# Placing other work in the gaps of each attention step by a table, and normalising the first batch on ScalarE

## The chip, the core and the metric

The kernel runs on one core of a Trainium2 chip. The core has five engines with a queue of their own each: TensorE (PE) for matmuls, with its weight loads (PEld) beside them, VectorE (DVE), ScalarE (ACT), GpSimd (POOL) and SyncE (SP), which here only issues DMAs. Each works off its instructions in the order in which the program holds them, and waits on semaphores for what others produce. The metric is the device time of the kernel in microseconds, as the median of several runs.

## What is computed

A linear attention with decay, whose output is laid out as 4 batches of 768 rows by 512 columns, goes through a Fourier mix, a normalisation and two dense layers. Cut to what matters:

```python
# q, k, v: (4, 8, 768, 64); blocks of 64 rows; lam: one decay per head
for b in range(nb):
    intra = einsum(qb, kb) * Dmask            # within a block
    intra = einsum(intra, vb)
    inter = einsum(qb * lam_pow, kv_state)    # from the state
    out[block] = intra + inter
    kv_state = lam_block * kv_state + einsum(kb * rev_pow, vb)
x = out.transpose(0, 2, 1, 3).reshape(4, 768, 512)

mixed = real(fft(fft(x, axis=1), axis=2))
u = x + mixed
un = (u - mean(u)) / sqrt(var(u) + 1e-6)      # over the 512 columns
out = u + maximum(un @ w_ch1, 0) @ w_ch2      # w_ch1: 512 x 2048, w_ch2: 2048 x 512
```

All is in 32 bit floats, but the two weight matrices arrive as 64 bit floats.

## The kernel before

**Attention** runs in 12 steps of 256 rows, three to a batch. A step first makes the scores of its rows (`scores`, L429 on TensorE; VectorE multiplies them by the decay, L435) and the part that comes from the state (`from_state`, L444). Then it transposes keys and queries of the next step (`turn_k` L394, `turn_q` L400, copied out of PSUM by ScalarE at L395 and L401, and scaled by VectorE at L403), turns the output of the step before back into rows (`back`, transposes at L470), updates the state (`to_state`, L409 and, on VectorE, L419) and makes the part within the blocks (`within`, L450, copied out by ScalarE at L456). `attention` is a Python generator: it yields three times in a step, so that other work can be written into the program at these places: behind the scores and ahead of the next transposes, behind these and ahead of `back`, and behind `within` and ahead of the next scores. Below they are the first, second and third gap.

**The mix** of a batch (`fft_ln`) has folds of mirrored rows and columns on VectorE (L598 to L692), matmuls along the sequence (L725, five products of eight TensorE records), and for each of three groups of two row tiles a product along the width (`wide`, L737 to L742), sums of it into the rows (`summed`, L818 to L825), means and variances (`stats`, L756 and L757 on VectorE, L760 and L761 on GpSimd), the normalising (`norm`, L777 on VectorE) and transposes of the normalised rows for the dense layers (L784, copied out at L788). One group ends with one more product for a single row (`width(HC, ...)`). The first batch (`LEADS`) is folded from tiles that attention leaves in SBUF; the others are read back through DRAM, with mirrored rows by gathers (L612, L619).

**The weights** come in 32 chunks of 512 KB. A chunk is converted from 64 to 32 bits by five VectorE instructions (L264, L266, L269, L272, L273) with one of ScalarE among them (L265), in three parts with a yield behind each. Chunks 0 to 7 are the first half of the columns of `w_ch1`, chunks 8 to 15 the half of `w_ch2` that goes with it; then follows the second half.

**The dense layers** of a group and a half of the hidden units (`mlp`) are eight units of four matmuls each for the first layer (L882; the Relu on ScalarE at L890, in the second half every other one on VectorE at L888), and then the second layer (L896), added into the rows at L926 and L927 for the first half and L930 and L931 for the second.

**The order.** Up to `strict[0] = False` instructions marked by `P` or `keep` stay on their engine in the order in which the Python code writes them. It writes attention, the first batch's mix and the weights' conversion as a mixture by weights (`mixed`): each generator has a length in made-up units, and the one that is furthest behind its share goes next. Behind attention come eight first-layer units of group 1 and then eight of group 2, with the rest of the first half of the weights between them. From `strict[0] = False` on a scheduler in the build orders the instructions by its own estimates, within the dependences. The last part (`late`, behind the release of the pools) works on the remaining eight groups and isn't touched.

## Time and profile before

| | |
|---|---|
| median of 3 runs | 786.39 us (785.94 to 786.59) |
| profiled execution | 785.49 us, span 783.6 us |
| granted TensorE clock, mean | 0.993 |
| ScalarE, GpSimd busy | 200.9 us, 189.3 us |
| DMA | 123.49 MB, mean 158 GB/s |

In the rows below a line of a timeline has start, length, engine, source line, operation, output and inputs with their shapes, the number of instructions merged into it, and in brackets the idle time ahead of it with what ended it. A line of a table by stretches has the stretch and its length, then for PE, PEld, DVE, ACT and POOL the busy time with the number of instructions, then the clock that TensorE was granted (1 is full speed), the busy share of the DMA and its GB/s. A line of groups has the busy time and the mean in ns of one instruction, and behind the second bar the idle time ahead of them.

### The profile page before, as it was taken

How to read it: one execution, taken by the hardware profiler on the slowest of the kernel's cores; microseconds unless marked ns; L12 is line 12 of the kernel's file. 1: busy time of each engine (PE TensorE's matmuls, PEld its weight loads, DVE VectorE, ACT ScalarE, POOL GpSimd, SP SyncE). 2: the span in 40 equal slices, each digit the busy share in tenths (PEclk: the TensorE clock that was granted, in tenths of full speed). 3: DMA queues.
4: the chain of work that ended last, by engine and by line, in shares of the span. 5: the costliest groups of instructions: out<-in, count | busy, mean ns of one | idle time of the engine just before them, and what ended most of it. 6: DMA issues, size and time to landing. Idle time of an engine off the chain costs nothing.

```text
span 783.6 us, 17057 instructions
## 1 busy us (share of the span) xinstructions
PE 742.9 (95%) x6872; PEld 645.0 (82%) x6872; DVE 612.8 (78%) x1183; ACT 200.9 (26%) x468; POOL 189.3 (24%) x215
## 2 busy tenths in 40 slices
PE   6899987699999999999899999999999999999997
PEld 5788876587576758659746889999999999999997
DVE  5689866687998858556884999889986699758983
ACT  2454443343132111002101221024311442024310
POOL 3343442310002114210102970360014100230013
PEclk9999999899999999999999999999999999999999
DMA  9879885174352536530350464876545455465442
GB/s 213 249 199 240 228 240 145 47 278 135 86 194 78 96 119 196 121 121 27 68 147 28 148 223 142 264 248 212 173 138 157 151 178 175 129 182 176 138 144 68
DMA packets 132739, 123.49 MB, mean 158 GB/s; under 512 B 67006, under 2 KB 93246, under 8 KB 132662
## 3 DMA queue, kind: packets, MB, share of 16 engines
q1 hardware_dynamic: 126326, 101.56, 45.9%
q0 software_dynamic: 4032, 12.99, 4.7%
q10 hardware_dynamic: 2304, 7.87, 3.1%
q8 instruction: 54, 0.88, 0.5%
q14 instruction: 23, 0.19, 0.1%
HBM read 90.66 MB, written 31.73 MB: 156 GB/s over the span
## 4 chain that ended last, share of the span: by engine, by line
PE 68%; DVE 17%; issue 7%; DMA 4%; POOL 3%; ACT 1%; SPq 0%; DVEq 0%; POOLq 0%; ACTq 0%
PE p L1331 21%; PE p L1257 17%; PE pm L896 7%; PE pm L882 7%; PE p L1164 5%; PE pa L882 2%; PE pa L725 2%; DVE w L273 1%; DVE e L272 1%; DVE w L269 1%; DVE stt L756 1%; PE pa L450 1%; PE pa L429 1%; DMA w<-in_v_dram 1%; PE pm L725 1%
## 5 line engine op out<-in xcount | busy, mean ns | idle before, releaser
L896 PE MATMUL pm<-w,hr 128*128 128x512 f32 x240 | 104.6, 592 | 0.0
L882 PE MATMUL pm<-ut,w 128*128 128x256 f32 x432 | 97.7, 380 | 3.2 <-DVE hr L888 1.5
L882 PEld LDWEIGHTS pm<-ut,w 128*128 128x128 f32 x432 | 81.2, 190 | 18.1 <-issue 3.3
L896 PEld LDWEIGHTS pm<-w,hr 128*128 128x128 f32 x240 | 45.4, 190 | 53.4 <-issue 52.1
L1352 POOL TENSOR_TENSOR y<-y,u 128x512 f32<-128x512 f32 x12 | 19.9, 1661 | 186.8 <-DVE y L1361 155.5
L1331 PE MATMUL p<-tx,sx 128*128 128x128 f32 x400 | 52.7, 275 | 0.0
L1331 PEld LDWEIGHTS p<-tx,sx 128*128 128x128 f32 x400 | 48.6, 192 | 0.0
L1266 DVE TENSOR_TENSOR ha<-p,ha 128x512 f32<-128x512 f32 x60 | 40.1, 685 | 8.3 <-PE p L1257 8.1
L1337 ACT COPY y<-p 128x128 f32<-128x128 f32 x48 | 12.8, 266 | 103.6 <-PE p L1331 103.1
L1339 DVE TENSOR_TENSOR y<-p,y 128x128 f32<-128x128 f32 x92 | 25.6, 285 | 16.1 <-PE p L1331 9.4
L1331 PE MATMUL p<-w,ha 128*128 128x128 f32 x288 | 37.4, 275 | 0.0
L265 ACT ACTIVATE e<-e,cvt 128x512 uint16<-128x512 uint16 x32 | 22.9, 721 | 53.8 <-DVE e L264 53.7
L1266 DVE TENSOR_TENSOR hs<-p,hs 128x512 f32<-128x512 f32 x39 | 26.2, 685 | 12.0 <-PE p L1257 12.0
L1331 PEld LDWEIGHTS p<-w,ha 128*128 128x128 f32 x288 | 34.9, 192 | 0.1
L890 ACT ACTIVATE hr<-pm 128x256 f32<-128x256 f32 x34 | 13.0, 381 | 84.3 <-PE pm L882 83.4
L1257 PE MATMUL p<-sx,tx 128*128 128x128 f32 x264 | 33.9, 275 | 0.0
L871 POOL DMA_INDIRECT out_dram<-y,ix x12 | 13.6, 1130 | 76.0 <-DVE y L931 64.3
L1257 PEld LDWEIGHTS p<-sx,tx 128*128 128x128 f32 x264 | 31.6, 192 | 0.0
L429 PE MATMUL pa<-w 64*64 64x128 f32 x768 | 27.4, 277 | 3.9 <-issue 2.0
L429 PEld LDWEIGHTS pa<-w 64*64 64x64 f32 x768 | 23.5, 136 | 6.3 <-issue 3.2
L1257 PE MATMUL p<-ur,w 128*128 128x128 f32 x216 | 28.0, 275 | 0.0
L612 POOL DMA_INDIRECT fo<-xa,ix x6 | 7.1, 1182 | 86.3 <-PE pa L725 74.0
(334 smaller groups left out, 1923.1 us busy)
## 6 DMA issues: line engine op xcount, KB each, us to landing
tx<-td SPq DMA_DIRECT2D x84, 256.0 KB, 2.9
tx<-sd SPq DMA_DIRECT2D x63, 256.0 KB, 3.0
words<-in_moe_w_ch_dram SPq DMA_DIRECT2D x19, 512.0 KB, 4.2
raw<-in_moe_w_ch_dram ACTq DMA_DIRECT2D x13, 512.0 KB, 7.3
w<-in_v_dram SPq DMA_DIRECT2D x12, 512.0 KB, 4.4
words<-in_k_dram SPq DMA_DIRECT2D x11, 512.0 KB, 6.2
td<-tx SPq DMA_DIRECT2D x21, 256.0 KB, 2.0
ud<-x SPq DMA_DIRECT2D x16, 256.0 KB, 2.2
```

The costliest lines, as they stand in the source:

```text
L265: P(nc.scalar.activation(pw, pw, AF.Relu, bias=cvt[:, 0:1], scale=8.0))
L429: lead(P(mm(pss[r][hi][HD[ch], hp, :], lhsT=kT[HD[hi], r, hp, D * ch:D * ch + D], rhs=qT[HD[hi], hp, C * ch:C * ch + C], start=True, stop= ...
L725: mm = P(nc.tensor.matmul(ps[:, n, :], lhsT=piece(a, i, n), rhs=cs[0:rows, a, i in (2, 3), n, :], start=(a == 0), stop=(a == 1)))
L871: P(nc.gpsimd.indirect_dma_start(out=out_high, out_offset=row_of(2 + HC * (b + 1) + T - HC), in_=y[:, :], in_offset=None))
L882: P(nc.tensor.matmul(ps, lhsT=w1[:, c, 128 * fc:128 * fc + 128], rhs=ut[:, c, :], start=(c == 0), stop=(c == KO - 1)))
L896: return P(nc.tensor.matmul(ps, lhsT=hr[(fc - f0) // 4][:, fc % 4, 128 * i:128 * i + 128], rhs=w2[:, fc, :], start=(fc == f0), stop=(fc == ...
L1164: nc.tensor.matmul(ps, lhsT=s2.A[a][:, kt, 128 * i:128 * i + 128], rhs=U[b][:, kt, :], start=(first and kt == 0), stop=(kt == 1), skip_gro ...
L1257: nc.tensor.matmul(ps[:, 128 * i:128 * i + 128], lhsT=ab[m][0][:, 128 * i:128 * i + 128], rhs=ab[m][1], start=(start and i == 0), stop=Tru ...
L1266: V.tensor_tensor(o, p, o, op=ADD)
L1331: nc.tensor.matmul(ps[:, 0:HM // 2], lhsT=ab[m][0][i], rhs=ab[m][1][:, i, :], start=(start and i == 0), stop=(i == HF // 2 - 1), skip_grou ...
L1339: V.tensor_tensor(o, ps[:, 0:HM // 2], o, op=ADD)
L1352: nc.gpsimd.tensor_tensor(o, y, u, op=ADD)
```

## The change

Five things are changed.

- A table `PLAN` gives for each of the 12 steps three strings, one for each gap. Each letter writes one unit into the gap: `w` the next third of a weight chunk, `m` the next unit of the first batch's mix.
- A string `REST` does the same for the time behind attention; there `l` is a first-layer unit of group 1 and `k` one of group 2. Four `l`, four `k`, four `l` and four `k` stand in it, with the last units of the mix and 22 thirds of chunks between them; seven thirds follow.
- The first batch's mix yields in smaller units in an order of its own: the width product of a group ahead of the norm of the one before, and the norm of a tile and its transposes in two units.
- The first batch's rows are normalised by ScalarE (`activation` with Identity, a scale and a bias for each row) instead of VectorE. GpSimd makes the bias from mean and scale by two more instructions for each group.
- The copies of the first batch's rows out of PSUM in `back` go from VectorE to ScalarE, but for one tile.

```diff
@@ -490,8 +490,11 @@
                 if not last:
                     x = xn_[b, c] = new(xp, [C, DM], "x")
                     px = turned(oT[i], cols)
-                    P(nc.vector.tensor_copy(x[:, 0:HM], px[:, 0:HM]))
-                    P(nc.vector.tensor_copy(x[:, HM:DM], px[:, DM - 1:HM - 1:-1]))
+                    if n == 1 and ch == 0:
+                        P(nc.vector.tensor_copy(x[:, 0:HM], px[:, 0:HM]))
+                        P(nc.vector.tensor_copy(x[:, HM:DM], px[:, DM - 1:HM - 1:-1]))
+                    else:
+                        put(px, x)
                 continue
             inside = b == INSIDE
             x = new(xn, [C, DM], "xn") if inside and c >= HC else new(xp, [C, DM], "x")
@@ -707,7 +710,6 @@
         if b in LEADS:
             yield from fold_a(b)
             yield from fold_b(b, sets)
-            yield 2.0
         else:
             mirrors(b)
             yield 6.0
@@ -759,6 +761,11 @@
             rs = new(np_, [128, G], "rs")
             P(nc.gpsimd.tensor_scalar(ve, mv[:, :, 1], EPS, None, op0=ALU.add))
             P(nc.gpsimd.tensor_tensor(rs, ve, mhalf, op=ALU.pow))
+            if b in LEADS:
+                sh = new(np_, [128, G], "sh")
+                P(nc.gpsimd.tensor_tensor(sh, mv[:, :, 0], rs, op=ALU.mult))
+                P(nc.gpsimd.tensor_scalar(sh, sh, -1.0, None, op0=ALU.mult))
+                mv = sh
             chains[g] = mv, rs
 
         def norm(g):
@@ -774,6 +781,9 @@
                 u = xs[b, TT[g][i]]
                 with tc.high_priority(300) if (b, g) in PLAIN[1:3] else ExitStack():
                     for o, x in ((un[:, 0:HM], u[:, 0:HM]), (un[:, HM:DM], u[:, DM - 1:HM - 1:-1])):
+                        if b in LEADS:
+                            P(nc.scalar.activation(o, x, AF.Identity, bias=mv[:, i:i + 1], scale=rs[:, i:i + 1]))
+                            continue
                         P(nc.vector.tensor_scalar(o, x, mv[:, i, 0:1], rs[:, i:i + 1],
                                                 op0=ALU.subtract, op1=ALU.mult))
                 if plain and strict[0]:
@@ -813,8 +823,6 @@
             return ds, A
 
         def summed(t, ds, A):
-            if strict[0]:
-                yield 0.6
             P(nc.vector.tensor_tensor(even_odd(ds[:, 0:HM]), A, even_odd(odd[:, :]), op=ALU.subtract))
             P(nc.vector.tensor_tensor(even_odd(ds[:, HM + 1:2 * HM + 1]), A, even_odd(odd[:, :]), op=ALU.add))
             unread[0] = False
@@ -835,25 +843,56 @@
                                         x3[0:1, HM + 1:DM:2], op=ALU.add))
                 yield 0.9
 
+        if b in LEADS:
+            n1, n2, n0 = (norm(g) for g in (1, 2, 0))
+
+            def one(gen):
+                next(gen)
+                return 1.0
+
+            s = summed(1, *wide(1))
+            yield 1.0
+            yield one(s)
+            yield one(s)
+            s = summed(2, *wide(2))
+            yield 1.0
+            stats(1)
+            yield 1.0
+            yield one(n1)
+            yield one(n1)
+            yield one(s)
+            yield one(s)
+            yield one(n1)
+            yield one(n1)
+            s = summed(0, *wide(0))
+            yield 1.0
+            stats(2)
+            yield 1.0
+            yield one(s)
+            yield one(s)
+            yield one(n2)
+            yield one(n2)
+            yield one(s)
+            yield one(n2)
+            yield one(n2)
+            stats(0)
+            yield 1.0
+            for _ in range(4):
+                yield one(n0)
+            return
+
         now = wide(1)
         yield from summed(1, *now)
         stats(1)
-        yield 9.0 if b in LEADS else 4.0 if (b, 1) in PLAIN else 2.0
+        yield 4.0 if (b, 1) in PLAIN else 2.0
         for t, after in ((1, 2), (2, 0)):
-            if t == 1 and b in LEADS:
-                yield from norm(1)
             now = wide(after)
-            if t == 1 and b not in LEADS:
+            if t == 1:
                 yield from norm(1)
             yield from summed(after, *now)
-            if t == 2 and b not in LEADS:
+            if t == 2:
                 yield from norm(2)
             stats(after)
-        if b in LEADS:
-            yield from norm(2)
-            yield 1.5
-            yield from norm(0)
-            return
         yield 1.0
         yield from norm(0)
 
@@ -1518,25 +1557,33 @@
             yield d
 
     att, mix = attention(), fft_ln(0)
-    run(part(att, 0.1))
-    run(part(att, 9.0))
-    run(mixed((until(att, lambda: (0, 0) in xs), 20.0), (w, 2.0)))
-    run(mixed((mix, T_FOLD), (att, 3.6 * t_step), (w, 1.4)))
-    run(mixed((mix, 8.0), (att, 0.9 * t_step), (w, 1.6)))
-    run(mixed((mix, 30.0), (att, 3.2 * t_step), (w, 3.0)))
-    run(mix)
-
     half = [[mlp(b, g, h * FO // 2, (h + 1) * FO // 2) for b, g in PLAIN[:3]] for h in range(2)]
     half[0][0] = mlp(*PLAIN[0], 0, FO // 2, half[0][2])
     fr = chain([fft_ln(1), fft_ln(2), front_sums(), fft_ln(3)])
     t_half = 1.5 * t_mlp
     lead_half = chain(half[0])
-    run(mixed((att, 1.2 * t_step), (w, 2.0)))
+
+    PLAN = [("", "", ""), ("w", "", "w"), ("w", "w", "mm"),
+            ("mmw", "", "mmm"), ("mmm", "mm", "mmmm"), ("mmmm", "m", "mmm"),
+            ("mmmm", "mm", "mmw"), ("mw", "w", "mww"), ("mww", "mw", "mww"),
+            ("mw", "w", "mm"), ("mm", "m", "mmm"), ("mw", "mmmw", "mm")]
+    REST = "lmwlmwlmwlmwwmkmwkmwkwwkwwlmwlmwlmwlwkmwkwkwkwwww"
+    first_two = {"w": w, "m": mix, "l": part(lead_half, 13.5), "k": part(half[0][1], 13.5)}
+
+    def go(units):
+        for u in units:
+            next(first_two[u], None)
+
+    next(att)
+    for units in chain(PLAN):
+        next(att)
+        go(units)
     run(att)
     over[0] = True
     rest[:] = [0, 1, 2, 3, 4, 5, 6, 7]
-    run(mixed((part(lead_half, 13.5), 13.6), (w, 3.0)))
-    run(mixed((part(half[0][1], 13.5), 13.6), (w, NW / 2 - landed[0])))
+    go(REST)
+    for u in "mlk":
+        run(first_two[u])
     run(until(w, lambda: landed[0] >= NW // 2))
     strict[0] = False
     run(mixed((lead_half, t_half - 27.0), (fr, 62.0), (w, 0.5 * NW)))
```

The change moves rows on each engine. Three places are shown. In the new kernel's rows the source lines are shifted: L725 is L727, L737 to L742 are L739 to L744, L777 is L785 (ScalarE) or L787 (VectorE), L784 is L794, L818 and L819 are L826 and L827, L882, L890 and L896 are L921, L929 and L935.

The first is TensorE between the state products of the last step but one (L444) and the transposes for the last step (L394, L400). `un` is a normalised row tile of the first batch, `ys` the sequence products, `oT` attention's output. Before:

```order
L444 MATMUL pm_101<-w_146,st_140 64x128 x2
L738 MATMUL pm_102<-dt,ys_154 128x129
L739 MATMUL pm_102<-dt,ys_158 128x129
L740 MATMUL pm_102<-dt,ys_155 128x128
L784 MATMUL pm_103<-ident,un_2138 128x128 x4
L784 MATMUL pm_102<-ident,un_2146 128x128 x4
L394 MATMUL pa_96<-ident,w_147 128x128 x4
L394 MATMUL pa_97<-ident,w_147 128x128 x4
L400 MATMUL pa_98<-ident,w_147 128x128 x4
L400 MATMUL pa_99<-ident,w_147 128x128 x4
```

And in the changed kernel:

```order
L444 MATMUL pm_101<-w_146,st_140 64x128 x2
L739 MATMUL pm_102<-dt,ys_156 128x128
L740 MATMUL pm_102<-dt,ys_154 128x129
L741 MATMUL pm_102<-dt,ys_158 128x129
L742 MATMUL pm_102<-dt,ys_155 128x128
L744 MATMUL pm_102<-dt,ys_157 128x128
L394 MATMUL pa_96<-ident,w_147 128x128 x4
L394 MATMUL pa_97<-ident,w_147 128x128 x4
L400 MATMUL pa_98<-ident,w_147 128x128 x4
L400 MATMUL pa_99<-ident,w_147 128x128 x4
```

Two tiles of normalised rows no longer stand ahead of the last step's transposes; a width product does.

The second is ScalarE at the beginning of the first-layer units behind attention. `hr` is the output of a Relu, `e` the chunk's exponent words. Before:

```order
L265 ACTIVATE e_2407<-e_2407,cvt 128x512
L890 ACTIVATE hr_2416<-pm_102 128x256
L890 ACTIVATE hr_2416<-pm_103 128x256
L265 ACTIVATE e_2426<-e_2426,cvt 128x512
L890 ACTIVATE hr_2416<-pa_96 128x256
L890 ACTIVATE hr_2416<-pa_97 128x256
L265 ACTIVATE e_2444<-e_2444,cvt 128x512
```

And in the changed kernel, where `un` is normalised by ScalarE and `ut` is its transpose:

```order
L929 ACTIVATE hr_2334<-pa_96 128x256
L785 ACTIVATE un_2337<-x_625,sh_2249,rs_2246 128x256 x2
L929 ACTIVATE hr_2334<-pa_97 128x256
L798 COPY ut_2336<-pa_98 128x4x128
L929 ACTIVATE hr_2334<-pa_99 128x256
L265 ACTIVATE e_2365<-e_2365,cvt 128x512
L929 ACTIVATE hr_2334<-pm_101 128x256
L785 ACTIVATE un_2374<-x_827,sh_2249,rs_2246 128x256 x2
L798 COPY ut_2336<-pm_102 128x4x128
L929 ACTIVATE hr_2389<-pm_103 128x256
L265 ACTIVATE e_2406<-e_2406,cvt 128x512
```

The norms of group 2 and its copies now stand between the Relus, and there are more Relus to each conversion.

The third is VectorE at the second batch's first width sums, behind `strict[0] = False`, where the scheduler sets the order. Before:

```order
L266 TENSOR_SCALAR w_147<-words_148 128x512
L273 SCALAR_TENSOR_TENSOR w_147<-w_147,e_2847 128x512
L269 SCALAR_TENSOR_TENSOR w_147<-words_148,w_147 128x512
L266 TENSOR_SCALAR w_147<-words_149 128x512
L269 SCALAR_TENSOR_TENSOR w_147<-words_149,w_147 128x512
L818 TENSOR_TENSOR ds_2810<-pa_2802,bs 128x2x128
L819 TENSOR_TENSOR ds_2810<-pa_2802,bs 128x2x128
L824 TENSOR_TENSOR x_1023<-x_1023,ds_2810 128x512
L825 TENSOR_TENSOR x_2551<-x_2551,ds_2810 128x512
```

And in the changed kernel:

```order
L272 SCALAR_TENSOR_TENSOR e_2782<-words_148,e_2782 128x512
L269 SCALAR_TENSOR_TENSOR w_147<-words_148,w_147 128x512
L826 TENSOR_TENSOR ds_2815<-pa_2807,bs 128x2x128
L273 SCALAR_TENSOR_TENSOR w_147<-w_147,e_2782 128x512
L827 TENSOR_TENSOR ds_2815<-pa_2807,bs 128x2x128
L264 TENSOR_SCALAR e_2827<-words_149 128x512
L832 TENSOR_TENSOR x_1016<-x_1016,ds_2815 128x512
L833 TENSOR_TENSOR x_2556<-x_2556,ds_2815 128x512
L266 TENSOR_SCALAR w_147<-words_149 128x512
L272 SCALAR_TENSOR_TENSOR e_2827<-words_149,e_2827 128x512
```

Before, 30 of the 32 chunks were through their last step when the width sums came; now 27 are, and the rest stand among the sums, means and norms.

## The prediction

> **What bounds the kernel now.** I read the page's first part, then a table of busy time over stages cut at places that I found in TensorE's timeline, then the waits in both timelines.
>
> ```profile
> PE 742.9 (95%) x6872; PEld 645.0 (82%) x6872; DVE 612.8 (78%) x1183; ACT 200.9 (26%) x468; POOL 189.3 (24%) x215
> 0.00:67.90 67.90, 57.15 (x1329) 50.15 (x1329) 48.95 (x101) 28.04 (x62) 27.89 (x41) 1.00 0.90 225
> 67.90:162.30 94.40, 75.54 (x1573) 67.91 (x1574) 70.08 (x137) 40.67 (x95) 32.90 (x35) 0.95 0.63 174
> 162.30:190.00 27.70, 27.70 (x131) 24.39 (x130) 20.34 (x37) 11.42 (x27) 1.35 (x1) 1.00 0.64 215
> 190.00:260.00 70.00, 70.00 (x261) 44.62 (x259) 66.36 (x150) 17.48 (x40) 5.93 (x7) 1.00 0.42 126
> 260.00:420.00 160.00, 154.99 (x614) 108.39 (x614) 107.21 (x230) 17.81 (x54) 24.39 (x36) 1.00 0.40 105
> ```
>
> After the stretch's length come PE, PEld, DVE, ACT and POOL, then TensorE's granted clock and the DMA. TensorE is the bound: 95% busy over the span, full from 162.3 to 260. Its idle time lies almost all ahead of 162.3, in attention, and more than half of that between 67.9 and 162.3 (18.9 us, at a mean clock of 0.95). The change can win there and hardly elsewhere. The stretch 162.3 to 190 is the 16 units of first layers, 1.73 us each. But VectorE from 190 to 260 is busy 66.4 of 70 us: whoever brings TensorE there sooner meets VectorE.
>
> ```profile
> 113.39 1.97 PE L429 MATMUL pa<-w 64*64 64x128 f32 x62 [1.76 <-DVE w L403]
> 119.92 0.76 PE L784 MATMUL pm<-ident,un 128*128 128x128 f32 x4 [3.69 <-DVE un L777]
> 125.77 0.76 PE L784 MATMUL pm<-ident,e 128*128 128x128 f32 x4 [1.73 <-DVE e L777]
> 143.31 1.09 PE L784 MATMUL pm<-ident,un 128*128 128x128 f32 x4 [7.00 <-DVE un L777]
> 120.00:124.00 4.00, 4.00 (x20) 3.52 (x20) 0.35 (x2) 2.35 (x4) 0.00 (x0) 0.58 0.43 85
> 144.00:148.00 4.00, 3.49 (x17) 3.06 (x17) 0.73 (x2) 1.99 (x4) 0.06 (x1) 0.51 0.00 0
> ```
>
> Four waits make 14.2 us. Three are the transposes of the first batch's normalised rows (L784), which stand in TensorE's order ahead of attention's next transposes while the normalising (L777) is far back in VectorE's queue. Behind the two long ones the clock falls to 0.58 and 0.51 for a 4 us window: 1.7 us lost in each.
>
> **The change part by part.** The sum is made against the profiled execution: 785.49 us, span 783.6. It lies 0.9 below the median of the three runs, 786.39, and I add that at the end.
>
> *Attention to its end.* The same instructions are spread over the three gaps of each step. One step is a turn of the loop from L394 to the next L394.
>
> ```profile
> 58.50:67.90 9.40, 8.72 (x218) 8.10 (x217) 9.37 (x18) 4.33 (x11) 3.70 (x4) 1.00 1.02 255
> 89.90:105.80 15.90, 15.58 (x260) 14.45 (x258) 8.53 (x15) 8.20 (x20) 4.57 (x6) 1.00 0.84 224
> 105.80:120.50 14.70, 9.24 (x238) 8.47 (x237) 13.52 (x25) 4.96 (x11) 7.88 (x8) 1.00 0.84 229
> 120.50:145.80 25.30, 16.07 (x288) 14.32 (x287) 16.89 (x38) 8.15 (x20) 7.47 (x9) 0.84 0.29 84
> 145.80:162.30 16.50, 15.28 (x307) 13.33 (x306) 10.71 (x21) 9.59 (x22) 2.62 (x2) 0.94 0.36 121
> 91.61 2.79 PE L725 MATMUL pm<-cs,fe 128*128 128x193 f32 x16
> 100.77 0.39 PE L737 MATMUL pm<-dt,ys 128*128 128x128 f32 x2
> 101.66 0.39 PE L742 MATMUL pm<-dt,ys 128*128 128x128 f32 x2
> ```
>
> A step without matmuls of the mix takes 9.4 us (58.5 to 67.9); I use 9.5. A sequence product (L725, 16 records are two) costs 1.4, a width product 1.1 (five matmuls, the first at 100.77, the fifth at 101.66: 0.22 apart). In the new order the six intervals behind 67.9 hold: nothing; one sequence product; two; two and a width product; a width product; and the last interval a width product and two transposes. So 9.7 + 10.9 + 12.3 + 13.5 + 10.7, and for the last the 16.5 of before plus 1.1 less 1.2 for its slowed clock, 16.4. Attention ends at 67.9 + 73.5 = 141 instead of 162.3. Up to 67.9 I change nothing: the waits there stem from ScalarE's conversion step (L265) standing ahead of the L395 copies, and it stands there still.
>
> *First layers with the rest of the mix.* Behind attention now stand the 16 units (27.7 us), four tiles of transposes (0.7 each, by the 0.76 of L784's rows less their overlap), the one-row width product (0.7), and a new wait: ScalarE normalises (L785) between the Relus of these units.
>
> ```profile
> L890 ACT ACTIVATE hr<-pm 128x256 f32<-128x256 f32 x34 | 13.0, 381 | 84.3 <-PE pm L882 83.4 <-PE pa L896 0.8
> L480 ACT COPY x<-pa 128x256 f32<-128x256 f32 x11 | 4.2, 382 | 2.2 <-PE pa L470 2.2
> L265 ACT ACTIVATE e<-e,cvt 128x512 uint16<-128x512 uint16 x32 | 22.9, 721 | 53.8 <-DVE e L264 53.7
> L395 ACT COPY w<-pa 128x512 f32<-128x512 f32 x24 | 13.2, 585 | 24.6 <-PE pa L394 22.9 <-DVE w L435 1.7
> L788 ACT COPY ut<-pm 128x512 f32<-128x512 f32 x6 | 3.5, 590 | 16.0 <-PE pm L784 16.0
> ```
>
> L265 has one pointer operand and takes 136 ns longer than a copy of its width (721 against 585), so a 256 wide half with two pointers is between 0.38 (a copy) and 0.65; I take 0.55, nearest to L265's difference. At the second tile of group 2 TensorE has no other work in its order: Relu 0.38, two halves 1.1, signals 0.2, then after the transposes the copy (L788) 0.59 and 0.15 before the first unit of that group. That is 2.4 us (2.1 to 2.6). At the other three tiles a unit of 1.73 us stands between and hides it. [...]
>
> Sum: 27.7 + 2.8 + 0.7 + 2.4 = 33.6, so these units end on TensorE at 175 instead of 190: **15 us** won there.
>
> *The weights on VectorE.* This is where I expect a part to be given back.
>
> ```profile
> 185.96 0.69 DVE L272 SCALAR_TENSOR_TENSOR e<-words,e 128x512 uint16<-128x512 uint16 x1 [4.09 <-ACT e L265]
> 186.69 0.69 DVE L273 SCALAR_TENSOR_TENSOR w<-w,e 128x512 f32<-128x512 f32 x1
> 187.30 0.42 DVE L264 TENSOR_SCALAR e<-words 128x512 uint16<-128x512 uint16 x1
> 190.03 0.42 DVE L264 TENSOR_SCALAR e<-words 128x512 uint16<-128x512 uint16 x1
> 193.18 0.69 DVE L598 TENSOR_TENSOR fe<-fo,xn 128x512 f32<-128x512 f32 x1
> 240.24 0.42 DVE L818 TENSOR_TENSOR ds<-pa,bs 128x256 f32<-128x256 f32 x1
> 263.29 0.42 DVE L888 TENSOR_SCALAR hr<-pm 128x256 f32<-128x256 f32 x1
> 239.17 0.43 DVE L266 TENSOR_SCALAR w<-words 128x512 uint32<-128x512 uint32 x1 [0.37 <-DMA words<-in_moe_w_ch_dram]
> 244.90 0.74 DVE L777 TENSOR_SCALAR un<-x,mv,rs 128x256 f32<-128x256 f32 x2 [1.17 <-POOL rs L761]
> 247.41 0.69 DVE L272 SCALAR_TENSOR_TENSOR e<-words,e 128x512 uint16<-128x512 uint16 x1 [0.79 <-ACT e L265]
> 253.91 0.74 DVE L777 TENSOR_SCALAR un<-x,mv,rs 128x256 f32<-128x256 f32 x2 [1.14 <-POOL rs L761]
> 262.64 0.73 DVE L777 TENSOR_SCALAR un<-x,mv,rs 128x256 f32<-128x256 f32 x2 [1.16 <-POOL rs L761]
> 260.75 1.53 PE L882 MATMUL pm<-ut,w 128*128 128x256 f32 x6 [0.73 <-DVE mv L757]
> 288.18 0.59 PE L725 MATMUL pa<-cs,fe 128*128 128x193 f32 x2 [1.81 <-DVE fe L643]
> ```
>
> A chunk costs VectorE 2.73 us when nothing delays it (187.30 to 190.03). Before, the sixteenth (L273 at 186.69) was done 3 us ahead of TensorE's last unit. Now each chunk's ScalarE step stands in that queue behind the Relu of a given unit, so VectorE cannot run ahead: when the last unit ends, the thirteenth is half done. What then stands ahead of the second batch's first fold (L598) is the rest of it, four chunks and 1.3 more, 15 us: 190 instead of 193.2. From that fold to the first Relu on VectorE (L888) it took 70.1 us, 4.6 of them the five waits in these rows. In the new order the same conversions stand in that stretch, but some of them between the width sums and the norms, where the waits were, and one norm (0.7) goes behind the Relu. I take 64.8, so the Relu runs at 254.8 instead of 263.3: 8.5 us sooner, at worst 3.9 if the waits stay. TensorE waits for VectorE there (0.73 at 260.75, for a bank that is read just ahead of that Relu; some 7 now), and so of the 15 us **8 are left**.
>
> At 288 another wait goes: the third batch's folds stood behind the first final sums (L930, L931), because a gather into a freed buffer waited for these; now they stand ahead of them. Of its 1.81 I count 1. From there to the end the order is nearly the same, TensorE is busy 155.0 of 160 and 357.6 of 363.6 us, and what is won is carried through.
>
> ```profile
> 420.00:783.60 363.60, 357.56 (x2973) 349.50 (x2971) 299.85 (x531) 85.48 (x192) 96.81 (x96) 1.00 0.53 166
> ```
>
> Costed at nothing: row copies that go from VectorE to ScalarE in attention (0.38 each beside 9.5 us steps in which ScalarE is busy about half), and two more small GpSimd operations a group, off the path as long as a transposition comes a gap later.
>
> 785.5 - 8 - 1 + 0.9 = **777 us**.
>
> **The rivals.**
> 1. *VectorE holds more back* (0.20). The waits in its stretch stay: the Relu only 3.9 sooner, and nothing at 288. For it: 66.4 of 70 us busy. 786.4 - 3.9 = 782.5.
> 2. *VectorE doesn't hold* (0.17). Relus in the first layers come early enough that ScalarE lets the chunks through, and the second layers find their weights: the whole 15 stay and the 1 at 288, 770. Against it: the 4.09 wait at 185.96, the same queue with fewer things in it.
> 3. *VectorE paces the steps* (0.08, the slower end). What stands between an attention product and the next scores runs ahead of the four score multiplications (L435) that TensorE's next transposes wait for. The longest such pieces are 1.9 us (three of a chunk's operations). If VectorE's slack ahead of L435 were used up in all of the eleven later steps, 21 us would go, and 4 to 6 more as the late end pushes the weights: 791. It decides from 1.5 us a step on. Against it: in 58.5 to 67.9 VectorE was busy 9.37 of 9.40 us and the step still took 9.4.
>
> [...]
>
> **How the numbers follow.** The forecast has 0.50 (774 to 780), the rivals 0.20, 0.17 and 0.08; 0.05 is for no change through waits that I don't see. The range reaches over the first rival and most of the second: 769 to 785. Under 0.2%, some 1.6 us, is about what a measurement can't tell from no change. Faster: 0.86; same 0.06; slower 0.08.
>
> **What would show it.** Right: attention's last transposes (L470) near 141, no wait over 3 us on a transposition, clock 1.0 throughout; the last first-layer unit near 175; VectorE's sixteenth chunk only some 8 us later; and one wait of 4 to 8 us on TensorE for VectorE between 230 and 262. Wrong: steps over 11 us without sequence products (rival 3), or no such wait (rival 2).

## The result and the profile after

The changed kernel takes 778.84 us (median of four runs, 776.55 to 780.86) against 786.49 us before (four runs, 785.94 to 786.84): a ratio of 0.990, 95% interval 0.987 to 0.993. It is 1% faster. The prediction was 777 us (769 to 785). The profiled execution is the slowest of the four, 780.86 us, with a span of 779.1.

The first part of the page of after:

```profile
PE 744.9 (96%) x6872; PEld 644.2 (83%) x6872; DVE 604.6 (78%) x1163; ACT 208.5 (27%) x488; POOL 195.0 (25%) x221
```

VectorE has 8.2 us less (20 operations fewer) and ScalarE 7.6 us more. To see where time was won and lost I cut the program at four marks that both orders share: the start of attention's last transposes (L470), of the first second-layer product (L896, now L935), of the first product with combined weights (L1164, now L1203), and the end. The marks in TensorE's timeline of before:

```profile
161.31 1.15 PE L470 MATMUL pa<-ident,oT 128*128 128x128 f32 x8 [0.72 <-ACT oT L456]
189.91 2.31 PE L896 MATMUL pm<-w,hr 128*128 128x512 f32 x5
421.62 2.64 PE L1164 MATMUL p<-ur,w 128*128 128x256 f32 x10
```

And of after, with the waits that matter between them:

```profile
145.14 1.14 PE L470 MATMUL pa<-ident,oT 128*128 128x128 f32 x8 [2.85 <-ACT oT L456]
155.39 0.82 PE L794 MATMUL pm<-ident,un 128*128 128x128 f32 x3 [1.09 <-ACT un L785]
156.99 3.63 PE L921 MATMUL pm<-ut,w 128*128 128x256 f32 x8 [0.68 <-ACT ut L798]
180.38 4.03 PE L935 MATMUL pm<-w,hr 128*128 128x512 f32 x9
257.32 1.96 PE L921 MATMUL pm<-ut,w 128*128 128x256 f32 x8 [0.16 <-DVE x L966]
280.12 1.01 PE L727 MATMUL pa<-cs,fe 128*128 128x193 f32 x2 [2.90 <-DVE fe L646]
416.20 4.05 PE L1203 MATMUL p<-ur,w 128*128 128x256 f32 x18
```

The differences of these rows, in us; the last column is a second profile of the changed kernel (e1 below; its marks are 143.56, 178.81, 414.44 and 776.2):

| part | before | after | difference | predicted | difference in e1 |
|---|---|---|---|---|---|
| up to attention's last transposes | 161.31 | 145.14 | -16.2 | -21 | -17.8 |
| first layers with the rest of the mix | 28.60 | 35.24 | +6.6 | +5.9 | +6.7 |
| second layers, batches 2 and 3 | 231.71 | 235.82 | +4.1 | +6 | +3.9 |
| combined weights to the end | 361.98 | 362.90 | +0.9 | 0 | -0.2 |
| span | 783.6 | 779.1 | -4.5 | -9 | -7.4 |

The three waits of transpositions that were 12.4 us are gone from attention. Three shorter ones stand in their place, 2.85, 1.09 and 0.68 us. And at 280, where the prediction had 1 us to win, the wait grew from 1.81 to 2.90. Two of these places cost more than their wait, by TensorE's granted clock. Windows of after:

```profile
156.00:160.00 4.00, 3.33 (x10) 0.65 0.70 277
160.00:164.00 4.00, 4.00 (x19) 0.93 0.00 0
280.00:284.00 4.00, 3.88 (x10) 0.57 0.11 41
```

Behind the length and PE's busy time with its count stand the clock, the DMA share and GB/s. What the clock lacks to 1, times the 4 us of a window, gives 1.4 + 0.3 = 1.7 us lost in the first two windows and 1.7 in the third. VectorE is where it was predicted to be, behind:

```profile
188.78 0.69 DVE L273 SCALAR_TENSOR_TENSOR w<-w,e 128x512 f32<-128x512 f32 x1
195.27 0.68 DVE L601 TENSOR_TENSOR fe<-fo,xn 128x512 f32<-128x512 f32 x1
259.89 0.40 DVE L927 TENSOR_SCALAR hr<-pm 128x256 f32<-128x256 f32 x1
```

The first row is the last step of the sixteenth chunk, 8.4 us behind the mark of the first second-layer product, where the first-layer units end; the second the second batch's first fold, 14.9 behind it; the third the first Relu on VectorE. But TensorE hardly waits for it: 0.16 us at 257.32. That is the product for which it waited 0.73 us at 260.75 before.

### The profile page after: what moved, and what is told of

It is laid out like the page before. It is cut to its first block, busy times and chain, and to the rows that moved or that the text cites. A ratio compares the mean times of both kernels' runs of the same rounds, so it can differ in the third digit from the quotient of the medians.

```text
span 779.1 us, 17084 instructions
## 1 busy us (share of the span) xinstructions
PE 744.9 (96%) x6872; PEld 644.2 (83%) x6872; DVE 604.6 (78%) x1163; ACT 208.5 (27%) x488; POOL 195.0 (25%) x221
## 4 chain that ended last, share of the span: by engine, by line
PE 73%; DVE 9%; issue 7%; DMA 5%; POOL 3%; ACT 1%; SPq 0%; DVEq 0%; POOLq 0%; ACTq 0%
PE p L1370 21%; PE p L1296 17%; PE pm L935 7%; PE pm L921 7%; PE p L1203 5%; PE pa L921 2%; PE pa L429 2%; PE pa L727 2%; DMA words<-in_k_dram 1%; PE pa L450 1%; PE pa L400 1%; POOL fo L615 1%; PE pa L394 1%; PE pa L470 1%; DMA x<-xb,ix 1%
## 5 line engine op out<-in xcount | busy, mean ns | idle before, releaser
L935 PE MATMUL pm<-w,hr 128*128 128x512 f32 x240 | 106.5, 596 | 0.2 <-DVE w L273 0.2
L921 PE MATMUL pm<-ut,w 128*128 128x256 f32 x416 | 97.1, 386 | 3.3 <-ACT hr L929 2.4
L921 PEld LDWEIGHTS pm<-ut,w 128*128 128x128 f32 x416 | 78.4, 192 | 19.2 <-ACT hr L929 4.4
L935 PEld LDWEIGHTS pm<-w,hr 128*128 128x128 f32 x240 | 45.4, 191 | 51.7 <-issue 49.5
L1370 PE MATMUL p<-tx,sx 128*128 128x128 f32 x400 | 52.7, 275 | 0.0
L1370 PEld LDWEIGHTS p<-tx,sx 128*128 128x128 f32 x400 | 48.6, 192 | 0.0
L1370 PE MATMUL p<-w,ha 128*128 128x128 f32 x288 | 37.4, 275 | 0.0
L929 ACT ACTIVATE hr<-pm 128x256 f32<-128x256 f32 x32 | 12.3, 383 | 86.8 <-PE pm L921 85.1
L1370 PEld LDWEIGHTS p<-w,ha 128*128 128x128 f32 x288 | 34.9, 192 | 0.1
L429 PE MATMUL pa<-w 64*64 64x128 f32 x768 | 28.4, 284 | 5.2 <-issue 5.1
L615 POOL DMA_INDIRECT fo<-xa,ix x6 | 13.1, 2186 | 75.6 <-PE pa L727 69.9
L265 ACT ACTIVATE e<-e,cvt 128x512 uint16<-128x512 uint16 x32 | 22.9, 720 | 32.4 <-DVE e L264 32.2
L429 PEld LDWEIGHTS pa<-w 64*64 64x64 f32 x768 | 24.5, 140 | 7.8 <-issue 5.9
```

The lines of the kernel that those rows point to most:

```text
L265: P(nc.scalar.activation(pw, pw, AF.Relu, bias=cvt[:, 0:1], scale=8.0))
L429: lead(P(mm(pss[r][hi][HD[ch], hp, :], lhsT=kT[HD[hi], r, hp, D * ch:D * ch + D], rhs=qT[HD[hi], hp, C * ch:C * ch + C], start=True, stop= ...
L615: P(gather(out=eo[b][a][1][0:n, 1, 0:DM], out_offset=None, in_=xa[:, :], in_offset=row_of(a, n)))
L921: P(nc.tensor.matmul(ps, lhsT=w1[:, c, 128 * fc:128 * fc + 128], rhs=ut[:, c, :], start=(c == 0), stop=(c == KO - 1)))
L935: return P(nc.tensor.matmul(ps, lhsT=hr[(fc - f0) // 4][:, fc % 4, 128 * i:128 * i + 128], rhs=w2[:, fc, :], start=(fc == f0), stop=(fc == ...
L1370: nc.tensor.matmul(ps[:, 0:HM // 2], lhsT=ab[m][0][i], rhs=ab[m][1][:, i, :], start=(start and i == 0), stop=(i == HF // 2 - 1), skip_grou ...
```

## The experiments

My theory after the result: the time comes from the order, in which a transposition follows its normalising a gap later; what was not won is a few waits and the lowered clock behind them; and VectorE takes nothing back. The rivals: ScalarE wins by taking the normalising; the weight conversions that VectorE still owes when the first layers end cost the 4 us behind them; those 4 us are TensorE's own order. Ratios are to runs of the kernel before on the same chip, which took 784.5, 787.6 and 786.7 us (medians) beside the three groups of four runs.

**e1: the changed kernel again.**

> The changed kernel unaltered, on another chip, as the base for the runs beside it and to see where its four times (776.6 to 780.9) part. Theory (they part late, where TensorE waits for transfers): all landmarks up to 250 us (attention's last transposes, the last unit of the first layers, the second batch's first sequence product at 218.5, the first second-layer product at 249.4) within 0.5 us of the first profile, the difference behind 420. Rival (they part early, by the granted clock in the stretch 146 to 180, 0.95 in the first profile): the last first-layer unit 1 us or more away from 180.5 in this profile, and the clock with it. Time 776.5 to 781 in both.

Measured: 777.83 us, ratio 0.991 (0.989 to 0.993). Neither expectation held. The two profiles part early, but ahead of 145 and not by the clock in 146 to 180. A row of e1's timeline has a wait that the first profile lacks,

```profile
117.94 1.89 PE L409 MATMUL pa<-w,words 64*64 64x64 f32 x64 [2.68 <-DMA w<-in_v_dram]
```

and behind it the clock was 0.76 and 0.81 from 116 to 124, another 1.7 us. The first profile has three stops on L429 (1.51, 0.96 and 1.78 us) that e1 lacks or has shorter. The clock of the stretch 146 to 180 fell in both (0.65 and 0.93 from 156 to 164 in the first profile, 0.62 from 156 to 160 in e1). A second part of the spread is late, where the wait ahead of one product (L1370) is 1.76 us in the first profile and 0.66 in e1.

**e2: the three new waits taken away.**

```diff
-            ("mw", "w", "mm"), ("mm", "m", "mmm"), ("mw", "mmmw", "mm")]
-    REST = "lmwlmwlmwlmwwmkmwkmwkwwkwwlmwlmwlmwlwkmwkwkwkwwww"
+            ("mw", "w", "mm"), ("mm", "m", "mmm"), ("mw", "mmm", "wmm")]
+    REST = "lmwlmwlmmwlwwmlkmwkmwkwwkwwmwlmwlmwlwkmwkwkwkwwww"
```

> Takes away the three waits that the new order still has between 140 and 160 us: the weight unit of the last step's second gap goes behind that step's products, so that its ScalarE conversion no longer stands ahead of the row and oT copies (2.85 us at L470), and in the first layers the last one-row and normalising units come one unit earlier with a first-layer unit on either side of the transposes (1.09 and 0.68 us). All theories: attention's last transposes near 143.5 instead of 146.1, the last first-layer unit near 176 instead of 180.5. Theory A (VectorE paces 180 to 250, where it is 68.9 of 69.5 us busy): most is taken back there, the first second-layer product only 0 to 1.5 us sooner than in the unaltered change, time 777.5 to 779. Theory B (TensorE's own order sets the end there): 3.5 to 4.5 us sooner at that product, time near 775.

Measured: 772.42 us, ratio 0.984 (0.982 to 0.986), so 0.7% faster than the change itself. The cause of the 2.85 us wait can be read in ScalarE's timeline of after:

```profile
142.80 0.72 ACT L265 ACTIVATE e<-e,cvt 128x512 uint16<-128x512 uint16 x1 [2.70 <-DVE e L264]
143.43 0.35 ACT L480 COPY x<-pa 128x256 f32<-128x256 f32 x1
...
144.94 0.63 ACT L456 COPY oT<-pm 128x512 f32<-128x512 f32 x1
```

A conversion step (L265) stood ahead of the row copies and of the oT copies in ScalarE's queue, and waited for its first VectorE operation, which stood behind statistics. In e2's timeline the waits are 0.73 and 0.17, and the next two marks come early:

```profile
141.46 1.14 PE L470 MATMUL pa<-ident,oT 128*128 128x128 f32 x8 [0.73 <-ACT oT L456]
152.52 0.70 PE L921 MATMUL pm<-ut,w 128*128 128x256 f32 x2 [0.17 <-DVE w L273]
172.93 3.60 PE L935 MATMUL pm<-w,hr 128*128 128x512 f32 x8
408.49 3.83 PE L1203 MATMUL p<-ur,w 128*128 128x256 f32 x17
```

The first second-layer product comes 5.9 us sooner than in e1, the combined weights 5.95 sooner: the stretch between has 235.56 us, as in e1 (235.63), each with 1.7 us of lowered clock (0.66 and 0.92 from 272 to 280 in e2). All of the gain passed through. The waits make 3.7 us of it (2.85 less 0.73, and 1.77 less 0.17), the clock, which didn't fall at 156 in e2, another 1.7. The last 0.5 can't be put down to one cause, since ahead of these places e1 lost time to its transfer and e2 to a stop of 2.28 us on L429. Theory A falls as written: VectorE came earlier with TensorE (its first fold is at 187.82, again 14.9 us behind the last unit) and took nothing.

**e3: 2.75 us more on VectorE.**

```diff
+    for _ in range(4):
+        P(nc.vector.tensor_tensor(qpow, qpow, qpow, op=ALU.mult))
```

> Adds four VectorE products of 128x512 (0.69 us each by its other rows, 2.75 in all) that nobody reads, in VectorE's order behind the last unit of the first layers and ahead of the second batch's folds. Nothing else is altered. Theory A (VectorE paces 180 to 250): the first second-layer product comes 2 to 2.75 us later than in the unaltered change, time near 781.3. Theory B (TensorE paces): 0 to 0.7 us later, time 778.5 to 779.5.

Measured: 780.95 us (776.10 to 785.14 in 12 runs), ratio 0.995 (0.993 to 0.998). The stretch behind the first layers is 237.37 us without a lowered clock in it; less its 1.7 us of lowered clock it was 233.9 in e1. So the load costs 3.4 us in the profile, and 3.1 by the medians of e3 and e1. TensorE's timeline of e3:

```profile
261.19 1.97 PE L921 MATMUL pm<-ut,w 128*128 128x256 f32 x8 [2.40 <-DVE x L966]
```

This is the wait that the prediction had expected of the change itself. VectorE is at its edge there: what is added costs in full. The change itself stops just short of it, with 0.16 us.

**e4: normalising back on VectorE, in the new order** (excerpt; GpSimd's two operations for the bias go too).

```diff
-                        if b in LEADS:
-                            P(nc.scalar.activation(o, x, AF.Identity, bias=mv[:, i:i + 1], scale=rs[:, i:i + 1]))
-                            continue
```

> The changed order kept, but the first batch normalised by VectorE as before (12 operations of 0.37 us, 4.4 in all, go from ScalarE back to VectorE, and the two extra GpSimd operations of a group go). Theory O (the win is the order: transposes one gap behind the normalising): no wait over 1.5 us on a transposition in attention, attention's last transposes at 146 within 1 us, time 779 to 781. Theory S (ScalarE carries a share, since VectorE's queue holds the normalising behind the four score products and the weights): waits of 1.5 us or more on transpositions (L794) for VectorE, attention ends 2 us or more later and VectorE has 4.4 us more ahead of the second batch's folds, time 782 to 785.

Measured: 777.79 us, ratio 0.991 (0.989 to 0.993), as the change. In attention no transposition waits for a normalised tile, and behind it one waits 0.23 us where ScalarE made it wait 1.09. TensorE's timeline of e4:

```profile
156.97 0.76 PE L786 MATMUL pm<-ident,un 128*128 128x128 f32 x4 [0.23 <-DVE un L779]
```

Attention's last transposes start at 145.96, within theory O's 1 us, though a transfer (2.39 us at 119.22) and 3.13 us on ScalarE's oT copies stand ahead of them. In the new order it doesn't matter measurably who normalises: theory O.

**e5: an earlier gather** (on top of e2).

```diff
-                    uq = new(ep, [128, DM], "e")
+                    uq = new(fp, [128, DM + 4], "ds")[:, 0:DM] if (b, g, i) == (1, 0, 0) else new(ep, [128, DM], "e")
```

> On top of e2_tail_rest: the first transposed tile of the second batch's last group (L802) is written to another buffer, so that it no longer waits for a weight conversion's buffer, the last normalising of that batch (L787) runs ahead of the third batch's folds on VectorE, and the gather that needs its rows' buffer starts some 6 us sooner. Theory G (the wait of 2.6 to 2.9 us at the third batch's first sequence product, with the clock lowered to about 0.6 for 4 us behind it, stems from that gather): wait under 0.7 us, no lowered clock there, the stretch from the first second-layer product to the first product with combined weights (L1203) 3 to 4.3 us shorter than 235.6, time 768 to 770. Rival (VectorE's folds themselves are late, the gather is hidden): wait 2 us or more, time 771.5 to 773.

Measured: 771.58 us, ratio 0.980 (0.978 to 0.983). GpSimd's two gathers of the third batch's rows in after:

```profile
262.56 1.33 POOL L622 DMA_INDIRECT x<-xb,ix  x1 [1.06 <-DVE un L787]
270.83 0.96 POOL L622 DMA_INDIRECT x<-xb,ix  x1 [6.95 <-DVE un L787]
```

and in e5, with the product behind them:

```profile
256.19 1.06 POOL L622 DMA_INDIRECT x<-xb,ix  x1 [1.05 <-DVE un L787]
257.93 0.96 POOL L622 DMA_INDIRECT x<-xb,ix  x1 [0.67 <-DVE un L787]
269.53 0.59 PE L727 MATMUL pa<-cs,fe 128*128 128x193 f32 x2 [1.64 <-DVE fe L646]
300.68 3.70 PE L935 MATMUL pm<-w,hr 128*128 128x512 f32 x8 [1.17 <-DVE hr L927]
```

The gather was late as theory G said: it waited 6.95 us for a row buffer that is read by a normalising (`un`, L787), and that stood behind folds of the next batch. But its share in the wait was only 1.0 us (2.63 in e2, 1.64 here), and a new one of 1.17 took that back. The stretch has 233.96 us, 1.6 less than in e2, and that is the clock: 272 to 276 was at 0.66 in e2 and is at 1.00 in e5.

**e6: weights sooner** (on top of e2).

```diff
-    REST = "lmwlmwlmmwlwwmlkmwkmwkwwkwwmwlmwlmwlwkmwkwkwkwwww"
+    REST = "lmwlmwlmmwlwwmlkmwwkmwwkwwkmwwlmwwlmwwlwwkmwwkwwkwwkww"
```

> On top of e2_tail_rest: from the fifth first-layer unit on, two thirds of a weight chunk stand behind every unit (27 weight units in the first layers instead of 22). Theory W (the weight conversions that VectorE still owes when the first layers end, 14.3 us of them, make the stretch behind some 4 us longer than before): the sixteenth chunk 9 to 12 us after the first second-layer product instead of 14.3, the stretch to L1203 1.5 to 3 us shorter than 235.6, time 769.5 to 771. Rival (ScalarE's queue: each conversion step stands behind a Relu, and VectorE gets no further by an earlier place): sixteenth chunk still 13.5 us or more behind, time 772 to 774.

Measured: 772.61 us (769.04 to 778.59), ratio 0.982 (0.978 to 0.986), no gain over e2. The 14.3 us in the expectation was the eighteenth chunk by mistake; the sixteenth is 8.4 us behind in e2 and, at 176.19 against a mark of 172.46, 3.7 in e6. So VectorE did come 4.7 us sooner, and the stretch is no shorter: 237.10 us, of which 3.3 are a clock of 0.50 and 0.68 from 268 to 276. The rest, 233.8, is what e2 has without its lowered clock. e6 also has a new wait of 1.75 us for VectorE (L966) at 207.02, so by itself it says less against theory W than e7 does.

**e7: a part of the conversions left out** (L269 and L272 of chunks 11 to 15, so these weights are not converted right; the first of the two is shown).

```diff
-        P(nc.vector.scalar_tensor_tensor(dst, lo, 2.0 ** -32, d, op0=ALU.mult, op1=ALU.add))
+        if not 11 <= j < 16:
+            P(nc.vector.scalar_tensor_tensor(dst, lo, 2.0 ** -32, d, op0=ALU.mult, op1=ALU.add))
```

> The unaltered change, but of the chunks 11 to 15 the VectorE operations L269 and L272 are left out (ten of 0.6 us each, about 6.3 us), so these five weight chunks are not converted right. Theory W (VectorE's debt of conversions costs the stretch from the first second-layer product to the first product with combined weights 4 us): this stretch 232 to 233.5 us instead of 235.6 to 235.8, and time 775 to 776. Rival (its length is set by the order on TensorE and by the gather at 280): 235 to 236, time 777.5 to 778.5.

Measured: 778.54 us (four runs, 775.17 to 782.66), ratio 0.991 (0.987 to 0.994), as the change. The stretch has 233.96 us without a lowered clock, as e1 and e2 have when theirs is taken off (233.95, 233.9), and e5, which has none (233.96). With 6 us less on VectorE (by the mark it is 3.2 us less far behind, the fold 11.7 instead of 14.9), TensorE starts the third batch's sequence product 1.9 us sooner after the mark than in e1, behind a longer wait, and has lost this again at the next mark:

```profile
275.86 0.59 PE L729 MATMUL pa<-cs,fe 128*128 128x193 f32 x2 [3.22 <-DVE fe L648]
```

Theory W falls.

**e8: row copies back on VectorE.**

```diff
-                    if n == 1 and ch == 0:
+                    if True:
```

> The unaltered change, but the row copies that went to ScalarE are back on VectorE. Theory (they are hidden on either engine): attention's last transposes within 0.7 us of the unaltered change apart from waits for transfers, time within 1.5 us of 777.8. Rival (VectorE paces the steps of attention, ScalarE doesn't): a later end by 1.5 us or more and new waits for VectorE (L435 or L403), time 779.5 or more. Other rival (ScalarE's queue was the one that made the 2.85 us wait ahead of the last transposes): an earlier end by 1 to 2 us, since its two copies no longer stand ahead of the oT copies.

Measured: 778.97 us, ratio 0.989 (0.985 to 0.992), as the change, and the 2.85 us wait unchanged. Attention's last transposes start at 142.36, 1.2 us ahead of e1, but e1 lost that and more to its transfer, so this says little. The copies are hidden on either engine, and two of them made no difference behind the conversion step.

**e9: ScalarE's normalising alone, in the old order** (excerpt; GpSimd's operations for the bias come with it).

```diff
+                        if b in LEADS:
+                            P(nc.scalar.activation(o, x, AF.Identity, bias=mv[:, i:i + 1], scale=rs[:, i:i + 1]))
+                            continue
```

> The kernel before, with one part of the change alone: the first batch normalised by ScalarE, in the old order. Theory O (the order is what wins): the three long waits of transpositions in attention stay (3.69, 1.73 and 7.00 us before, 12.4 together; 9 or more here), because the statistics they need still stand far back in VectorE's queue; time 0.992 to 1.004 of before. Theory S (ScalarE wins by taking the normalising off VectorE's queue): these waits 5 us or less together, attention ends 7 us or more sooner, time under 0.992 of before.

Measured: 781.01 us, ratio 0.993 (0.990 to 0.995): most of the win, in the old order, though the intervals overlap. TensorE's timeline of e9 where before had 3.69, 1.73 and 7.00 (four of six waits shown):

```profile
116.62 0.93 PE L792 MATMUL pm<-ident,un 128*128 128x128 f32 x4 [0.85 <-ACT un L783]
120.67 0.92 PE L792 MATMUL pm<-ident,e 128*128 128x128 f32 x4 [1.37 <-ACT e L783]
133.39 0.93 PE L792 MATMUL pm<-ident,un 128*128 128x128 f32 x4 [2.00 <-ACT un L783]
...
145.05 1.12 PE L792 MATMUL pm<-ident,un 128*128 128x128 f32 x4 [1.67 <-ACT un L783]
157.16 1.15 PE L470 MATMUL pa<-ident,oT 128*128 128x128 f32 x8 [0.66 <-ACT oT L456]
```

The time is in theory O's range, the waits lie between the two theories. The long ones are shortened, but six short ones make 8.6 us in all, 1.56 of them for VectorE. Attention ends 4.2 us sooner, not 7. With e4 this says that the two parts overlap: the order removes the waits, ScalarE alone shortens them, and ScalarE adds nothing measurable to the order.

**e10: all units of a step in one gap.**

```diff
+    PLAN = [('', '', ''), ('', '', 'ww'), ('', '', 'wwmm'), ('', '', 'mmwmmm'), ('', '', 'mmmmmmmmm'), ('', '', 'mmmmmmmm'), ('', '', 'mmmmmmmmw'), ('', '', 'mwwmww'), ('', '', 'mwwmwmww'), ('', '', 'mwwmm'), ('', '', 'mmmmmm'), ('', '', 'mwmmmwmm')]
```

> The unaltered change, but with all units of an attention step in its third gap, ahead of the next scores, instead of in three gaps; same units, same count a step. Theory O (a unit on TensorE finds its operand ready only if a gap lies between it and the unit that makes it): waits of TensorE in attention grow by 5 us or more, on transpositions (L794) and on the score products behind folds and width sums on VectorE (L429), attention ends near 150 to 155 us, time 0.998 to 1.008 of before. Rival (only the move of the last tiles behind attention counts, the gaps don't): attention ends within 2 us of 143.5 to 145, time 0.988 to 0.993 of before.

Measured: 791.83 us, ratio 1.006 (1.004 to 1.008), slower than before. Rows of TensorE and two windows:

```profile
52.59 1.94 PE L394 MATMUL pa<-ident,w 128*128 128x128 f32 x8 [2.27 <-DVE w L435]
97.80 1.94 PE L394 MATMUL pa<-ident,w 128*128 128x128 f32 x8 [3.27 <-DVE w L435]
```

```profile
52.00:56.00 4.00, 3.41 (x16) 0.57 1.19 273
100.00:104.00 4.00, 4.00 (x35) 0.53 0.04 8
```

With a step's units in a row ahead of the score multiplications (L435) the next transposes wait for these: seven waits at L394, 12.9 us in all, against 0.2 in after. The clock falls behind the longer ones. It costs 12 us by the ratios. I had expected the waits at L794 and L429, and an end of attention near 150 to 155; its last transposes start at 158.41. The rival of this run falls too: the last tiles stand behind attention here as well, and nothing is won. This is the mechanism of the prediction's third rival, VectorE pacing the steps; the three gaps are what keeps it out.

**e11: eight and eight instead of four, four, four, four.**

```diff
-    REST = "lmwlmwlmwlmwwmkmwkmwkwwkwwlmwlmwlmwlwkmwkwkwkwwww"
+    REST = "lmwlmwlmwlmwwmlmwlmwlwwlwwkmwkmwkmwkwkmwkwkwkwwww"
```

> The unaltered change, but with the eight first-layer units of the first group ahead of the eight of the second, the mix's units between them at the same places, instead of four, four, four, four. Theory: the split in two parts costs or gains nothing by itself; since the second tile's transposes are now followed by a unit that doesn't need them, the 0.68 us wait goes and the 1.09 stays, first layers 33.5 to 34.5 us, time 0.988 to 0.992 of before. Rival (the split is needed, because the Relu or the buffers of eight open units hold TensorE up): new waits of TensorE in 146 to 180 of 2 us or more, time 0.993 or more.

Measured: 777.27 us, ratio 0.987 (0.983 to 0.990). The 0.68 us wait went, the 1.09 stayed, and first layers take 34.30 us, 1.7 of them a clock of 0.57 at 144 to 148. The split in two parts is worth nothing measurable here.

**e12: a width sum in two gaps** (on top of e5).

```diff
-            ("mw", "w", "mm"), ("mm", "m", "mmm"), ("mw", "mmm", "wmm")]
+            ("mw", "w", "m"), ("mmm", "m", "mmm"), ("mw", "mmm", "wmm")]
```

> On top of e5_early_gather: the second half of the first width sum (L832, L833 on VectorE) goes one gap later, behind the next four score multiplications (L435) instead of ahead of them. Theory (VectorE's piece of 2.2 us ahead of L435 makes the wait of 1.25 to 2.28 us at L429 near 124): that wait under 0.5 us, attention's last transposes 1 us sooner, time 0.5 to 1 us under e5_early_gather's ratio of 0.980. Rival (the statistics and so the first normalised tile then come too late): a new wait at the next L794 of 0.7 us or more, no gain.

Measured: 770.07 us, ratio 0.978 (0.975 to 0.980), the fastest of all, 2.2% under before; but its interval overlaps e5's, and the profiles reach the first second-layer product at the same 174.03 us. The stop at L429 is still there:

```profile
124.24 0.76 PE L429 MATMUL pa<-w 64*64 64x128 f32 x18 [1.69 <-issue]
```

VectorE's multiplications now start 2.0 us ahead of the stop's end, in after 1.3, and the stop is as long (1.78 in after, 1.25 in e5), so the piece of VectorE that was moved (L832, L833) isn't its cause. The theory of this run falls.

## Why the prediction was right, and where its steps were not

**Attention: the mechanism right, the size not: 21 us expected, 16 to 18 measured.** The three long waits are gone, no transposition in attention waits for a normalised tile for more than 0.3 us, and in the first profile the clock holds 1.00 up to 145. What was missed is the 2.85 us on ScalarE's queue: I had named the conversion step ahead of ScalarE's copies as a cost that stays up to 67.9, and did not look for it at the new end, where a weight unit had been put ahead of the last step's copies. e2 moves that unit and has the 2 us. By steps, from L394 to the next L394 and the last to the first first-layer product, the forecast has 9.7, 10.9, 12.3, 13.5, 10.7 and 16.4 us, the first profile 10.66, 11.34, 11.52, 13.74, 13.17 and 18.30. The last is the one with the 2.85. The fifth holds 2.6 us of waits that the sum didn't have, 1.78 of them a stop on L429 without a releaser and 0.82 for L403, the first another such stop of 1.51. The fifth step is over the 11 us that the prediction named as a sign of its third rival, but that rival's wait, for L435 ahead of L394, is 0.2 us in the whole profile. A reading of the prediction was too small as well: behind the 7.00 us wait of before two windows were lowered, 0.64 from 140 and 0.51 from 144, and not one.

**First layers: right but for the clock.** The new wait was put at 2.4 us and is 1.77 (1.09 and 0.68). In the groups of after the normalising of one half takes 597 ns,

```profile
L785 ACT ACTIVATE un<-x,sh,rs 128x256 f32<-128x256 f32 x10 | 5.4, 597 | 0.0
```

and a pair of halves, which overlap, 1.08 to 1.12 us, as assumed; one half had been put at 0.55. For the signals the sum had 0.2 and 0.15 us with no row to show them; in after they take 0.06 each: the second half ends at 155.82 and its transposes' weight load starts at 155.88, the copy ends at 156.93 and the product starts at 156.99. For the clock the sum counts nothing at this wait, and before doesn't show that: there the clock held 1.00 behind waits of 1.73 to 1.81 us and fell behind 3.69 and 7.00. Here it was 0.65 and 0.93 from 156 to 164, 1.7 us lost in the first profile, and as much in e1, e7 and e8. So 28.6 us became 35.2 instead of 34.5.

**VectorE holds 7 of the 15 us back: this step failed.** Its own figures were right: the fold stands 14.9 us behind the last unit (15 predicted), and from it to the first Relu it takes 64.6 us (64.8). What was wrong is the next step, that TensorE must then wait 4 to 8 us for that Relu: TensorE meets VectorE there with 0.16 us. No such wait was the prediction's own sign of being wrong here. In effect the sum had TensorE come to this product as far behind the mark of the first second-layer product as before, 70.8 us. It comes 76.9 us behind it: 2.0 us of that are waits, and TensorE is busy for 74.95 us on the way instead of 70.11, with 277 records instead of 262, since in the scheduler's order more products stand ahead. The first Relu on VectorE is 6.1 us further behind the mark too (79.5 instead of 73.4), so the two still meet. Why the scheduler's order came out so wasn't tried.

In e2 everything up to the first layers' end comes 5.9 us sooner and nothing is taken back. VectorE's place goes with the first layers: its first fold stands 14.9 us behind the mark in nine profiles (after, e1, e2, e4, e5, e8, e10, e11 and e12), whose marks lie between 172.93 and 195.70. The first Relu on VectorE comes 79.5 us behind the mark in after and e1, 82.9 in e3, 77.8 in e7 and 75.7 in e6; the stretch less its lowered clock has 233.9 us in e1, 237.4 in e3, 234.0 in e7 and 233.8 in e6. So later costs in full and sooner wins nothing, which is why I was misled: VectorE is full (37.79 of 38.10 us busy behind the mark in after), and full isn't late.

**The 4.1 us that the stretch did grow** have another source. From the first second-layer product to the second batch's first sequence product, TensorE in before and after:

```profile
189.91:226.01 36.10, 36.10 (x105) 19.76 (x104) 36.10 (x83) 8.25 (x16) 0.00 (x0) 1.00 0.42 125
180.38:218.48 38.10, 36.91 (x106) 19.51 (x105) 37.79 (x84) 8.63 (x16) 0.00 (x0) 1.00 0.43 131
```

Practically the same products (105 and 106 records) take 2.0 us more, and 38.1 in e1, e2, e4, e5, e8 and e12 too. Three waits make 1.2 of it:

```profile
186.81 1.13 PE L935 MATMUL pm<-w,hr 128*128 128x512 f32 x2 [0.25 <-DVE w L273]
...
214.18 1.99 PE L921 MATMUL pm<-ut,w 128*128 128x256 f32 x8 [0.47 <-ACT hr L929]
...
216.65 1.99 PE L921 MATMUL pm<-ut,w 128*128 128x256 f32 x8 [0.47 <-ACT hr L929]
```

The other 0.8 are in PE's busy time. In e9, with the old order behind attention, the whole stretch has 231.1 us (185.77 to 416.90), as before, and by e7 it isn't the conversions that VectorE owes. That leaves the order that came out for these units; which of its rules made it so wasn't tried. Of the remaining 2.1 us the clock at 280 makes 1.7; the longer wait there covers the rest.

**At 288 a win of 1 us: wrong in sign.** The folds did come ahead of the final sums, as I said. But a gather that they need then waited for a buffer that the last normalising reads, and TensorE's wait grew by 1.1 us. e5 shows that the gather makes only about 1 us of it; what makes the rest isn't settled.

**The number** is near by luck in part, because errors cancel. In the profile 5.5 us less were won up to the second layers than predicted, and 1.9 less given back behind them; with 0.9 at the end that is -4.5 instead of -9. The profiled run is the slowest of four: e1 has -7.4, the medians -7.65. The second rival has the outcome behind the first layers right: TensorE keeps what it wins there, and waits only 0.25 us for a weight. Its reason was wrong, since the conversions came through no earlier than the forecast said (8.4 us behind), and so was its size for attention.

**The parts of the change.** The order with its gaps carries it: 0.991 with the normalising on VectorE (e4), 1.006 with the gaps run together (e10). The table for attention and the string behind it were not tried apart. ScalarE's normalising alone gives 0.993 in the old order (e9) and nothing measurable on top of the new one. The row copies (e8) and the split of the first layers (e11) give nothing measurable.

## What to carry to other kernels

When an engine is busy all through a stretch, ask what its place in that stretch is tied to before you charge it for coming late: add a known load, take one away, and bring the stretch forward, as e3, e7 and e2 do. Where one queue serves two masters, look at what stands ahead of the path's instruction at every place where the order changed, above all at the ends: one weight unit moved by one gap, and first-layer units on either side of a transposition, were worth 0.7%, almost as much as the whole change (1%). And give every chain (sum, statistics, normalising, transposing) a gap of other work between its links; which engine does a link then matters little (777.79 us in e4, 777.83 in e1).
